# Attention tiles in a fused attention and MoE kernel: scores of one tile and the value product of the tile ahead in one run of small matmuls

## The chip, the core and the metric

The kernel runs on one core of a Trainium2 chip. The metric is the device time of one execution in microseconds, as a median over runs. The engines are PE (TensorE, matmuls and transposes; its weight loads are shown as PEld), DVE (VectorE), ACT (ScalarE), POOL (GpSimd) and SP, which here only issues DMAs. Each engine takes its instructions in the order of its own queue and waits on semaphores.

## What is computed

Chunked softmax attention, a dense MoE-like layer with a sigmoid-gated activation, and a layer of eight experts with routing:

```python
# q, k, v: (8, 8, 576, 64); chunks of 64 along the sequence
scores = scale * np.matmul(q_c, k_c.transpose(0, 1, 2, 4, 3))
scores = scores - np.max(scores, axis=-1, keepdims=True)
attn = np.exp(scores)
attn = attn / (np.sum(attn, axis=-1, keepdims=True) + 1e-09)
out = np.matmul(attn, v_c)
# x: (4608, 512), w_in (512, 2048), w_out (2048, 512)
h = x @ w_in
g = h * (1.0 / (1.0 + np.exp(-1.702 * h)))
x = g @ w_out
# routing: tokens with x @ w_skip > 0 go through their argmax expert
h = np.maximum(xc[mask] @ w1[e], 0.0)
y[mask] = gate_w[mask, None] * (h @ w2[e])
out[do_compute] = xc + y
```

## The kernel before, in words

The 4608 tokens are worked in nine blocks of 512 (NB = 9). A block's attention is four tiles of 128 tokens, each with two chunks and eight heads. The attention of block 0 is a prologue; that of block j + 1 runs inside the main loop of block j, between the big matmuls of the first MoE.

The main loop of a block has 16 steps (NF). Step i takes the 12 matmuls of `hps` (emit_h, line 269: 128x512, three products for each of four slices, as each operand is split into a high and a low part, xh and xl), then tanh on ACT and `sg` on DVE, `gh` on ACT and `gl` on DVE (emit_g), and the 12 matmuls of `yps` of the step ahead (emit_y, lines 289 to 293). Two banks of PSUM hold `hps`, four `yps`, and two, of the tag "at", all that attention and routing need. At a seam of two blocks the four `yps` are copied out as x2 by ACT and DVE (evac_y) and written to memory by SP, and x1, the attention's result, is split into xh (ACT casts) and xl (DVE) for the next block (split_x1). In a block's first eleven steps DVE also takes 36 dot products for the routing of the block ahead (line 326); late in the block a rank matmul `rk` takes a bank "at" (line 361). In block 0, `tick` converts the MoE weights from 64-bit numbers, on ACT, DVE and POOL.

A tile of attention has four stages in class Att: `a` transposes q and k (qTp and kTp, copied to qT and kT by ACT), `b` multiplies the scores (line 153, 16 products of 64x64, each two instructions in the trace) into two banks, `s0` and `s1`; DVE takes the maxima and the differences from these banks, and ACT the exp. `c0` normalises on DVE and `c1` transposes to pT. `d` is the product with the values (line 196, again 16 products) into two banks, `pv0` and `pv1`, from which ACT copies to x1. In the scores the bank is that of the operands' half of the rows; in the product too.

A table sets at which of the 16 steps a stage is emitted: STEPS = (0, 1, 3, 4), plus three for each further tile of the block (STEPS0 in block 0). `load_qk` of a tile is issued behind stage `a` of the tile ahead and `load_v` behind its stage `d`. The written order is not the final one: a scheduler of the framework orders the instructions of each engine by dependences and its own costs, so that a stage may move some steps, or be split with big matmuls in its middle.

Of the kernel before, what the change touches and what calls it, by code (L numbers as in the profile page):

```python
# [21 lines left out]
def kernel(  # L22
# [17 lines left out]
    NT, DM = out.shape  # L40
    DFF = w_in.shape[1]
    NE, _, FF = w1.shape
    P = 128
    CH = 64
    NHP = H // 2
    KD = DM // P
    NF = DFF // P
    BT = 512
    TPB = BT // P
    NB = NT // BT  # L50
# [7 lines left out]

    STEPS0 = (0, 1, 4, 5)
    STEPS = (0, 1, 3, 4)
    NXT = NT // SL + NE + NSING + 2
    BIG = float(1 << 20)

# [12 lines left out]
    def bank(shape, tag, name):  # L78
        return pp.tile(shape, F32, tag=tag, name=name, bufs=PB[tag])
# [28 lines left out]
    class Att:  # L108
# [34 lines left out]
                self.T.append(sb)  # L143

        def b(self):
            qT, kT = self.T
            ps = [bank([P, NHP, CH], self.tags[1], f"s{h2}") for h2 in range(2)]
            for hp in range(NHP):
                for c in range(2):
                    for h2 in range(2):  # L150
                        r = slice(h2 * CH, (h2 + 1) * CH)
                        cc = slice(c * CH, (c + 1) * CH)
                        PE.matmul(ps[h2][cc, hp, :], qT[r, hp, cc], kT[r, hp, cc], start=True, stop=True)

            self.p = qT.rearrange("p j (g k) -> p j g k", g=2)
            pw = self.p.rearrange("p (x h) g k -> p h g x k", h=2)
            self.st = ap.tile([P, NHP, 2], F32, tag="st", name="st", bufs=2)
            for h2 in range(2):
                DVE.tensor_reduce(self.st[:, :, h2], ps[h2], axis=AX.X, op=ALU.max)
            for h2 in range(2):  # L160
                DVE.tensor_tensor(
                    pw[:, h2], ps[h2].rearrange("p (g x) k -> p g x k", g=2),
                    self.st[:, :, h2:h2 + 1].rearrange("p (g x) o -> p g x o", g=2).to_broadcast(
                        [P, 2, 2, CH]), op=ALU.subtract,
                )
            ACT.activation(out=self.p, in_=self.p, func=AF.Exp, scale=float(D) ** -0.5)
# [15 lines left out]
            ACT.copy(out=self.pT, in_=ps)  # L182

        def d(self):


            ps = [bank([P, 2, P], self.tags[3], f"pv{g}") for g in range(2)]
            for x in range(2):
                for c in range(2):
                    for h2 in range(2):  # L190
                        for g in range(2):
                            r = slice(g * CH, (g + 1) * CH)
                            o = slice(h2 * CH, (h2 + 1) * CH)
                            cc = slice(c * CH, (c + 1) * CH)
                            j = 2 * x + h2
                            PE.matmul(ps[g][o, x, cc], self.v[r, c, j, :], self.pT[r, j, cc],
                                      start=True, stop=True)
            for g in range(2):
                ACT.copy(out=self.x1[g][:, :, self.col:self.col + P], in_=ps[g])


    whi, wlo = {}, {}
# [104 lines left out]
    def gate_load():  # L307
        SP.dma_start(out=wgT[:, :, 0:NE], in_=w_gate.rearrange("(k p) e -> p k e", p=P))
# [179 lines left out]
    def first_row(s):  # L488
        src = emeta[0:1, 1, s:s + 1] if s < NFIRST else meta[0:1, 0, s - NFIRST:s - NFIRST + 1]
        return SP.value_load(src, min_val=0, max_val=NROW - SL)  # L490
# [14 lines left out]
    def load_next():  # L505
        if cnt["load"] < len(wq):
            s, n, w = wq[cnt["load"]]
            cnt["load"] += 1
            single = s >= NFIRST + NPAIR and w == 0
            raw2.append((s, n, w, None if single else load_w2(expert(s), n, w)))  # L510
# [109 lines left out]
    def new_x1():  # L620
        return [mp.tile([P, 2, BT], F32, tag="x1", name="x1", bufs=2) for _ in range(2)]
# [22 lines left out]
    x1 = new_x1()  # L644
# [53 lines left out]
    xh, xl = split_x1(x1)  # L698

    fill, late = [], []  # L700
    wg = ws = None
    A = None
    slots = [Slot(s % 2, 2 if s < NFIRST + NPAIR else 1) for s in range(NS)]
    for j in range(NB):
        lastb = j + 1 == NB
        steps = {}
        if not lastb:
            x1 = new_x1()
            An = [Att((j + 1) * TPB + t, x1, t * P, ("at",) * 4, att_buf) for t in range(TPB)]
            for t in range(TPB):  # L710
                for n, kind in zip(STEPS if j else STEPS0, "abcd"):
                    steps.setdefault(3 * t + n, []).append((kind, t))
            if j == 0:
                An[0].load_qk()
                An[0].load_v()
            else:
                An[0].q, An[0].k, An[0].v = nxt_in
        else:
            rs.close()
            rawp = rs.enter_context(tc.tile_pool(name="raw", bufs=2, side="right", reuse_waits="tile"))  # L720
            for _ in range(4):
                load_next()
        ys = [bank([P, DM], "y", "yps") for _ in range(TPB)]
        prev = None
        nf = len(fill)
        for i in range(NF):
            steps.get(i, []).sort(key=lambda s: "acdb".index(s[0]))
            for kind, t in steps.get(i, ()):
                if kind == "c":
                    An[t].c0()  # L730
            sg = emit_h(i, xh, xl)
            span = NF // 2 - 2 if lastb else NF - 5
            nfill = -(-len(fill) // (span - i)) if i < span else 0
            if nfill:
                fill.pop(0)()
                nfill -= 1
            if j == 0:
                tick()
                if i == 7:
                    gate_load()  # L740
                elif i == 11:
                    gate_rows()
            g = emit_g(sg)
            if prev is not None:
                emit_y(i - 1, prev, ys)
            for kind, t in steps.get(i, ()):
                getattr(An[t], {"a": "a", "b": "b", "c": "c1", "d": "d"}[kind])()
                if kind == "a":
                    if t + 1 < TPB:
                        An[t + 1].load_qk()  # L750
                    elif j + 2 < NB:
                        nA = Att((j + 2) * TPB, None, 0, None, None)
                        nA.load_qk()
                elif kind == "d":
                    if t + 1 < TPB:
                        An[t + 1].load_v()
                    elif j + 2 < NB:
                        nA.load_v()
                        nxt_in = (nA.q, nA.k, nA.v)
            if j == 0:  # L760
                tick()
            for _ in range(nfill):
                fill.pop(0)()
            if late and (i >= span or late[0][0] < j):
                late.pop(0)[1]()
            if lastb:
                if prev is not None:
                    conv_next2()
                if i == NF // 2:
                    gstack.close()  # L770
                    m2 = ctx.enter_context(tc.tile_pool(name="m2", bufs=1, reuse_waits="tile"))
                    for s in range(NEARLY):
                        slots[s].list(first_row(s))
                if i >= NF // 2 + 2 and i - NF // 2 - 2 < NEARLY:
                    slots[i - NF // 2 - 2].gather((NB - 1) * BT)
            prev = g
        if j == 0:
            while tick_n[0] <= 2 * NF:
                tick()
            fstack.close()  # L780
            gstack = ExitStack()
            gp = gstack.enter_context(tc.tile_pool(name="gates", bufs=1, reuse_waits="tile"))
            wg = gp.tile([P, NE, DM], F32, name="wg")
            ws = gp.tile([P, DM], F32, name="ws")
            SP.dma_start(out=ws, in_=w_skip.rearrange("(o d) -> o d", o=1).to_broadcast([P, DM]))
            SP.dma_start(
                out=wg, in_=wgd[0:NE].rearrange("(o e) d -> o e d", o=1).to_broadcast([P, NE, DM]))
        if not lastb:
            xhn = split_x1(x1)
            emit_y(NF - 1, prev, ys)  # L790
            xh, xl = xhn
        else:
            slots[0].trans()
            emit_y(NF - 1, prev, ys)
            conv_next2()
        xs = evac_y(j, ys)
        lg = new_lg()
        if not lastb:
            fill = [lambda t=t, e=e, lg=lg, xs=xs: dot(lg, xs, t, e) for t in range(TPB) for e in range(NE + 1)]
            rt = route(j, lg)  # L800
            if j == NB - 3:
                rt.insert(3, order)
            late += [(j + 1, f) for f in rt]
# [108 lines left out]
```

## Time and profile before

| | us |
|---|---|
| median of 3 runs | 1247.73 (1245.55 to 1248.74) |
| profiled execution | 1246.55 |
| its span, first to last instruction | 1244.7 |
| PE busy (7984 matmul instructions) | 1194.9, 96% of the span |
| PE weight loads | 990.4 |
| DVE busy | 793.3 |
| ACT busy | 489.0 |
| POOL busy | 145.4 |

The busy time of an engine is a sum over stages that have different limits. The matmuls are pipelined: one that is shown with 0.39 us starts 0.23 us behind the one ahead of it, so it is the distance of the starts that tells what PE costs. "Idle before" in square brackets is time in which the engine stood still, with what released it.

### The profile page before, as it was taken

To read this page: it belongs to the slowest core of one execution; us is meant where nothing else is said; L and a number is where in the kernel's file an instruction comes from. 1 tells how busy PE (TensorE), PEld (TensorE's weight loads), DVE (VectorE), ACT (ScalarE), POOL (GpSimd) and SP (SyncE) were. 2 spreads that over 40 slices of the span, in tenths; PEclk is the share of its full clock that TensorE was granted. 3 is DMA by queue.
4 is the path that set the end of the run, shared out by engine and by line. 5 is a ranking of instruction groups with operands and counts; after the bars stand their busy time and mean duration, and the time that the engine had idled before them with its cause. 6 is when DMAs were issued, how large, how long until landed. Compare 5 with 4: busy or idle time off the path is not lost. (4 is left out here: it accounts for less than half of the span.)

```text
span 1244.7 us, 20848 instructions
## 1 busy us (share of the span) xinstructions
PE 1194.9 (96%) x7984; PEld 990.4 (80%) x7984; DVE 793.3 (64%) x1771; ACT 489.0 (39%) x825; POOL 145.4 (12%) x137
## 2 busy tenths in 40 slices
PE   6788999999999999999999999999999999999995
PEld 4566788878878887887887887788788999999885
DVE  5999477388359439548737835944884686666431
ACT  5866433243333333334334233333434444544320
POOL 2344000010000001001001000000103023132120
PEclk9999999999999999999999999999999999999998
DMA  9755241131122114113113112310524667667540
GB/s 220 207 159 159 53 154 37 34 94 35 34 81 48 26 27 111 35 26 95 42 35 94 26 43 61 69 26 9 186 86 152 216 186 258 212 222 236 190 152 9
DMA packets 181846, 128.99 MB, mean 104 GB/s; under 512 B 122335, under 2 KB 155359, under 8 KB 181616
## 3 DMA queue, kind: packets, MB, share of 16 engines
q1 hardware_dynamic: 177072, 117.09, 33.2%
q0 software_dynamic: 4672, 10.54, 2.5%
q8 instruction: 64, 1.05, 0.4%
q14 instruction: 38, 0.31, 0.1%
HBM read 103.59 MB, written 25.04 MB: 103 GB/s over the span
## 5 line engine op out<-in xcount | busy, mean ns | idle before, releaser
L269 PE MATMUL hps<-xh,whi 128*128 128x512 f32 x576 | 228.7, 400 | 6.5 <-DVE sg L273 5.9
L289 PE MATMUL yps<-whi,gh 128*128 128x512 f32 x576 | 229.6, 399 | 3.3 <-ACT gh L279 3.3
L269 PE MATMUL hps<-xl,whi 128*128 128x512 f32 x576 | 227.7, 395 | 3.5 <-DVE xl L259 3.5
L269 PE MATMUL hps<-xh,wlo 128*128 128x512 f32 x576 | 226.7, 394 | 0.0
L273 DVE SCALAR_TENSOR_TENSOR sg<-sg,hps 128x512 f32<-128x512 f32 x144 | 98.3, 684 | 201.4 <-ACT sg L272 200.6
L290 PE MATMUL yps<-wlo,gh 128*128 128x512 f32 x576 | 226.5, 393 | 0.0
L272 ACT ACTIVATE sg<-hps 128x512 f32<-128x512 f32 x144 | 85.5, 598 | 258.0 <-PE hps L269 244.7
L326 DVE CUSTOM_DVE_ANT_0 junk<-x,wg 128x512 f32<-128x512 f32 x256 | 176.3, 689 | 4.8
L516 DVE TENSOR_TENSOR elo<-rawe,ehi 128x1024 fp32r<-128x1024 f32 x88 | 107.5, 1223 | 88.3 <-ACT ehi L515 88.0
L293 PE MATMUL yps<-whi,gl 128*128 128x512 f32 x576 | 156.8, 393 | 0.7 <-DVE gl L280 0.7
L515 ACT CAST ehi<-rawe 128x1024 fp32r<-128x1024 f32 x88 | 92.2, 1049 | 144.1 <-PE h2p L581 70.3
L269 PEld LDWEIGHTS hps<-xh,whi 128*128 128x128 f32 x576 | 108.2, 189 | 31.0 <-DVE sg L273 8.4
L269 PEld LDWEIGHTS hps<-xl,whi 128*128 128x128 f32 x576 | 108.7, 189 | 27.3 <-DVE xl L259 5.2
L289 PEld LDWEIGHTS yps<-whi,gh 128*128 128x128 f32 x576 | 108.2, 188 | 27.4 <-ACT gh L279 4.3
L280 DVE SCALAR_TENSOR_TENSOR gl<-sg,gh 128x512 fp32r<-128x512 f32 x144 | 102.3, 710 | 42.1 <-ACT gh L279 39.5
L279 ACT ACTIVATE gh<-sg 128x512 fp32r<-128x512 f32 x144 | 91.0, 632 | 96.0 <-DVE sg L273 80.2
L269 PEld LDWEIGHTS hps<-xh,wlo 128*128 128x128 f32 x576 | 108.6, 189 | 22.5
L379 POOL DMA_INDIRECT tab<-pr,pos x36 | 42.2, 1172 | 713.1 <-DVE bs L369 519.8
L293 PEld LDWEIGHTS yps<-whi,gl 128*128 128x128 f32 x576 | 107.0, 188 | 23.2 <-DVE gl L280 1.3
L290 PEld LDWEIGHTS yps<-wlo,gh 128*128 128x128 f32 x576 | 108.2, 188 | 21.4
L581 PE MATMUL h2p<-xT,ehi 128*128 128x256 f32 x640 | 117.4, 283 | 0.0
L581 PEld LDWEIGHTS h2p<-xT,ehi 128*128 128x128 f32 x640 | 102.0, 191 | 2.6
(170 smaller groups left out, 1511.6 us busy)
## 6 DMA issues: line engine op xcount, KB each, us to landing
rawe<-in_moe_w_dram SPq DMA_DIRECT2D x88, 512.0 KB, 3.6
v<-in_v_dram SPq DMA_DIRECT2D x144, 64.0 KB, 2.5
x2d<-x SPq DMA_DIRECT2D x36, 256.0 KB, 5.8
out_dram<-x SPq DMA_DIRECT2D x36, 256.0 KB, 5.6
q<-in_q_dram SPq DMA_DIRECT2D x32, 256.0 KB, 3.1
k<-in_k_dram SPq DMA_DIRECT2D x32, 256.0 KB, 3.9
raw<-in_moe_w_in_dram SPq DMA_DIRECT2D x16, 512.0 KB, 4.8
raw<-in_moe_w_out_dram SPq DMA_DIRECT2D x16, 512.0 KB, 3.7
```

The lines of the kernel that those rows point to most:

```text
L269: PE.matmul(ps, a, b[:, kk], start=(n == 0), stop=(n == 3 * KD - 1))
L272: ACT.activation(out=sg, in_=ps, func=AF.Tanh, scale=0.851)
L273: DVE.scalar_tensor_tensor(sg, sg, 1.0, ps, op0=ALU.add, op1=ALU.mult)
L279: ACT.activation(out=gh, in_=sg, func=AF.Copy, scale=0.5)
L280: DVE.scalar_tensor_tensor(gl, sg, 0.5, gh.bitcast(F32), op0=ALU.mult, op1=ALU.subtract)
L289: PE.matmul(ys[t], gh[:, cs], wh, start=first, stop=False)
L290: PE.matmul(ys[t], gh[:, cs], wl, start=False, stop=False)
L293: PE.matmul(ys[t], gl[:, cs], wh, start=False, stop=last)
L326: DVE.tensor_tensor_reduce(junk, xs[t], wg[:, e, :] if e < NE else ws, 1.0, 0.0, ALU.mult, ALU.add, lg[:, t, e:e + 1])
L515: ACT.copy(out=hi, in_=raw)
L516: DVE.tensor_tensor(lo, raw, hi.bitcast(F32), op=ALU.subtract)
L581: PE.matmul(ps[:, f], a[:, c], self.xT[:, b, kk], start=(m == 0), stop=(m == 3 * KD - 1))
```

## The change

Attention from block 1 on becomes one stream of 32 tiles, `St`, over all blocks. The stages `b` and `d` are each cut into their matmuls (`b_mm`, `d_mm`) and what reads the banks (`b_post`, `d_post`). A function `burst` takes two banks of tag "at", each with the scores of one tile in its first half and the value product of the tile ahead in its second half: first the product's matmuls, then the scores' matmuls, then max, difference and exp of the scores, then the copies to x1. Bursts stand at steps 1, 4, 7, 10 and 13 of block 0, and at 1, 5, 9 and 13 of the blocks 1 to 7. A tile's transposes `a` come one step ahead of its burst, `c0` and `c1` two steps behind it, and its product in the next burst, three or four steps behind. The last burst has a product alone. `load_qk` of the next tile is issued behind `a`, `load_v` behind a tile's own burst. Lines move by 1 to 27: line 153 becomes 158, 196 becomes 207, 199 becomes 212, 269 becomes 296, 289 to 293 become 316 to 320.

```diff
-    STEPS0 = (0, 1, 4, 5)
-    STEPS = (0, 1, 3, 4)
+
+    BURSTS = {0: (1, 4, 7, 10, 13)}
+    BURSTN = (1, 5, 9, 13)
...
         def b(self):
+            ps = [bank([P, NHP, CH], self.tags[1], f"s{h2}") for h2 in range(2)]
+            self.b_mm(ps)
+            self.b_post(ps)
+
+        def b_mm(self, ps):
             qT, kT = self.T
-            ps = [bank([P, NHP, CH], self.tags[1], f"s{h2}") for h2 in range(2)]
...
+    def burst(nxt, old):
+
+
+        both = [bank([P, 4 * P], "at", f"sv{g}") for g in range(2)]
+        sc = [t[:, 0:2 * P].rearrange("p (h k) -> p h k", h=NHP) for t in both]
+        pv = [t[:, 2 * P:4 * P].rearrange("p (x k) -> p x k", x=2) for t in both]
+        if old is not None:
+            old.d_mm(pv)
+        if nxt is not None:
+            nxt.b_mm(sc)
+            nxt.b_post(sc)
+        if old is not None:
+            old.d_post(pv)
...
+    NST = NT // P - TPB
+    St = [Att(TPB + n, None, n % TPB * P, ("at",) * 4, att_buf) for n in range(NST)]
+    round_of = {}
+    for j in range(NB - 1):
+        for i in BURSTS.get(j, BURSTN):
+            round_of[j * NF + i] = len(round_of)
+    St[0].load_qk()
...
-            steps.get(i, []).sort(key=lambda s: "acdb".index(s[0]))
-            for kind, t in steps.get(i, ()):
-                if kind == "c":
-                    An[t].c0()
+            R = j * NF + i
+            nc_ = round_of.get(R - 2)
+            if nc_ is not None and nc_ < NST:
+                St[nc_].c0()
...
+            na = round_of.get(R + 1)
+            if na is not None and na < NST:
+                St[na].a()
+                if na + 1 < NST:
+                    St[na + 1].load_qk()
+            if nc_ is not None and nc_ < NST:
+                St[nc_].c1()
+            kb = round_of.get(R)
+            if kb is not None:
+                if kb:
+                    St[kb - 1].x1 = x1
+                burst(St[kb] if kb < NST else None, St[kb - 1] if kb else None)
+                if kb < NST:
+                    St[kb].load_v()
```

Over the whole kernel PE has its 1152 products of this kind in 84 runs before and in 43 now (eight of them in the prologue, in both); the transposes of q, k and p stand in 112 pieces before and in 134 now. Three places show how the order changes.

PE, burst of step 13 in block 1 of the new kernel (`sv_2541` and `sv_2542` are its two banks; line 207 is the product, line 158 the scores):

```order
L207 MATMUL sv_2541<-qT,v 64x64 [waits DMAHW7_49,Activation_49]
L207 MATMUL sv_2541<-qT,v 64x64
L207 MATMUL sv_2541<-qT,v 64x64 [waits DMAHW1_49]
L207 MATMUL sv_2541<-qT,v 64x64 x5
L158 MATMUL sv_2541<-kT,qT 64x64 x3
L207 MATMUL sv_2542<-qT,v 64x64 [waits DMAHW0_49,DVE_49]
L207 MATMUL sv_2542<-qT,v 64x64
L207 MATMUL sv_2542<-qT,v 64x64 [waits DMAHW2_49]
L207 MATMUL sv_2542<-qT,v 64x64 x5
L158 MATMUL sv_2542<-kT,qT 64x64 x3
L158 MATMUL sv_2541<-kT,qT 64x64
L158 MATMUL sv_2542<-kT,qT 64x64
```

Product and scores follow each other without a big matmul between them; in the bursts of this step in six blocks eight products and three scores of one bank stand together, since the other bank waits for DVE's copy of `rk`, while in the other bursts the two banks mostly take turns.

PE at the seam of blocks 1 and 2: before, the last product of the block ahead (line 196), the transposes of the next tile and the first matmuls of the new block.

```order
L196 MATMUL pv_2535<-qT,v 64x64
L196 MATMUL pv_2536<-qT,v 64x64
L140 MATMUL qTp<-ident,q 128x128 [waits DMAHW5_49,Activation_49]
L140 MATMUL qTp<-ident,q 128x128 x3
L140 MATMUL kTp<-ident,k 128x128 [waits DMAHW6_49,Activation_49]
L140 MATMUL kTp<-ident,k 128x128 x3
L269 MATMUL hps<-xh,whi 128x512 [waits Activation_49]
L269 MATMUL hps<-xh,whi 128x512
L269 MATMUL hps<-xl,whi 128x512 [waits DVE_49]
```

The same place of the new kernel, from the last `yps` matmuls of the step ahead to the first matmuls of the new block:

```order
L316 MATMUL yps<-whi,gh 128x512
L317 MATMUL yps<-wlo,gh 128x512
L316 MATMUL yps<-whi,gh 128x512
L317 MATMUL yps<-wlo,gh 128x512
L320 MATMUL yps<-whi,gl 128x512 [waits DVE_49]
L320 MATMUL yps<-whi,gl 128x512 x3
L141 MATMUL qTp<-ident,q 128x128 x3
L296 MATMUL hps<-xh,whi 128x512 [waits Activation_49]
L296 MATMUL hps<-xh,whi 128x512 [waits DVE_49]
L296 MATMUL hps<-xl,whi 128x512 [waits DVE_49]
```

The product that x1 needs no longer stands right ahead of the first matmul that reads xh: it is in the burst of step 13, with 36 big matmuls behind it.

ACT around a copy to x1, in block 1, before (line 199 copies, 272 is tanh, 279 is gh):

```order
L279 ACTIVATE gh<-sg 128x512 [waits DVE_49]
L199 COPY x_1713<-pv_2351 128x2x128 [waits PE_49]
L199 COPY x_1714<-pv_2352 128x2x128 [waits PE_49]
L272 ACTIVATE sg<-hps 128x512 [waits PE_49,Activation_49]
L279 ACTIVATE gh<-sg 128x512 [waits DVE_49]
L166 ACTIVATE qT<-qT 128x512 [waits DVE_49,PE_49]
```

And now (line 212 copies, 173 is exp, 299 is tanh, 306 is gh):

```order
L306 ACTIVATE gh<-sg 128x512 [waits DVE_49]
L212 COPY x_1757<-sv_2074 128x2x128 [waits DVE_49,PE_49]
L173 ACTIVATE qT<-qT 128x512 [waits DVE_49,PE_49,Activation_49]
L212 COPY x_1758<-sv_2075 128x2x128
L299 ACTIVATE sg<-hps 128x512 [waits PE_49]
L306 ACTIVATE gh<-sg 128x512 [waits DVE_49]
```

The first copy waits for DVE as well as for PE, the exp of the tile's scores has come between the two copies, and tanh and gh stand behind all three.

## Rows read from the trace of the kernel before

**Rows 1.** Busy time (and instructions) of each engine in two stretches.
```profile
49.00:122.00 73.00, 63.13 (x376) 48.08 (x376) 70.62 (x102) 52.99 (x95) 29.65 (x21) 1.00 0.55 167
262.00:363.00 101.00, 99.26 (x716) 79.78 (x715) 63.80 (x169) 34.30 (x64) 5.35 (x6) 1.00 0.21 53
```

**Rows 2.** Timeline of PE: start, duration, line, tiles, count; a run of 32.
```profile
300.13 0.39 PE L269 MATMUL hps<-xh,wlo 128*128 128x512 f32 x1
...
301.72 0.39 PE L269 MATMUL hps<-xh,whi 128*128 128x512 f32 x1
302.04 0.69 PE L153 MATMUL s<-kT,qT 64*64 64x64 f32 x32
302.66 0.50 PE L269 MATMUL hps<-xl,whi 128*128 128x512 f32 x1
303.00 0.39 PE L269 MATMUL hps<-xh,wlo 128*128 128x512 f32 x1
```

**Rows 3.** Timeline of PE, a run of 8.
```profile
370.87 0.39 PE L269 MATMUL hps<-xh,whi 128*128 128x512 f32 x1
371.19 0.34 PE L153 MATMUL s<-kT,qT 64*64 64x64 f32 x8
...
371.80 0.39 PE L269 MATMUL hps<-xh,wlo 128*128 128x512 f32 x1
```

**Rows 4.** Timeline of PE, 16 score matmuls of one bank.
```profile
132.48 0.68 PE L153 MATMUL s<-kT,qT 64*64 64x64 f32 x16
133.09 0.73 PE L293 MATMUL yps<-whi,gl 128*128 128x512 f32 x2
```

**Rows 5.** Timeline of PE, the last product, partly one bank at a time.
```profile
870.27 0.86 PE L196 MATMUL pv<-qT,v 64*64 64x64 f32 x32
871.06 1.20 PE L293 MATMUL yps<-whi,gl 128*128 128x512 f32 x4
```

**Rows 6.** Timeline of PE, scores and product in one run.
```profile
74.34 0.27 PE L153 MATMUL s<-kT,qT 64*64 64x64 f32 x2
74.35 0.27 PE L196 MATMUL pv<-qT,v 64*64 64x64 f32 x1
```

**Rows 7.** Timeline of PE, four transposes between big matmuls.
```profile
313.45 0.39 PE L269 MATMUL hps<-xh,wlo 128*128 128x512 f32 x1
313.69 0.60 PE L180 MATMUL pTp<-ident,qT 128*128 128x128 f32 x4
...
314.35 0.40 PE L269 MATMUL hps<-xl,whi 128*128 128x512 f32 x1
```

**Rows 8.** Waits of PE, 122 to 885 us: total, times, longest.
```profile
PE hps L269 <- DVE sg L273: 3.6, 8, 1.0
PE hps L269 <- DVE xl L259: 3.5, 4, 1.1
PE hps L269 <- ACT xh L258: 0.6, 1, 0.6
PE qTp L140 <- ACT x L199: 0.5, 1, 0.5
```

**Rows 9.** Busy times as in rows 1, then granted clock; behind the last seam.
```profile
874.00:878.00 4.00, 3.48 (x9) 2.75 (x10) 3.97 (x9) 0.88 (x2) 2.66 (x1) 0.58 0.61 213
```

**Rows 10.** Timeline of PE, ACT and DVE behind a run of scores.
```profile
249.92 0.60 ACT L272 ACTIVATE sg<-hps 128x512 f32<-128x512 f32 x1 [3.77 <-PE hps L269]
250.38 0.50 PE L289 MATMUL yps<-whi,gh 128*128 128x512 f32 x1
...
251.16 0.75 DVE L159 TENSOR_REDUCE st<-s 128x4 f32<-128x256 f32 x2
...
251.27 0.63 ACT L279 ACTIVATE gh<-sg 128x512 fp32r<-128x512 f32 x1 [0.76 <-DVE sg L273]
...
251.82 0.75 DVE L161 TENSOR_TENSOR qT<-s,st 128x256 f32<-128x256 f32 x2
```

**Rows 11.** Groups of DVE instructions, 122 to 870 us: busy us, mean ns.
```profile
L326 DVE CUSTOM_DVE_ANT_0 junk<-x,wg 128x512 f32<-128x512 f32 x224 | 154.3, 689 | 4.3
```

More of the change, by code (lines that the diff above doesn't have):

```diff
@@ L153, in b, with b_post @@
                         PE.matmul(ps[h2][cc, hp, :], qT[r, hp, cc], kT[r, hp, cc], start=True, stop=True)
-            self.p = qT.rearrange("p j (g k) -> p j g k", g=2)
+        def b_post(self, ps):
+            self.p = self.T[0].rearrange("p j (g k) -> p j g k", g=2)
             pw = self.p.rearrange("p (x h) g k -> p h g x k", h=2)
@@ L187, in d, with d_mm @@
             ps = [bank([P, 2, P], self.tags[3], f"pv{g}") for g in range(2)]
+            self.d_mm(ps)
+            self.d_post(ps)
+        def d_mm(self, ps):
             for x in range(2):
@@ L197, in d, with d_post @@
                                       start=True, stop=True)
+        def d_post(self, ps):
             for g in range(2):
                 ACT.copy(out=self.x1[g][:, :, self.col:self.col + P], in_=ps[g])
+    def burst(nxt, old):
[9 more added lines that the diff above has]
+            old.d_post(pv)
     whi, wlo = {}, {}
@@ L705 @@
         lastb = j + 1 == NB
-        steps = {}
         if not lastb:
             x1 = new_x1()
[L709 to L717, printed above, removed]
         else:
@@ L745 @@
                 emit_y(i - 1, prev, ys)
[L746 to L759, printed above, removed]
+            na = round_of.get(R + 1)
[12 more added lines that the diff above has]
+                    St[kb].load_v()
             if j == 0:
```

## Prediction

> **What bounds the kernel now.** I read the page's busy times first, which the table ahead gives: PE, the matmul engine, is busy for nearly all of the span. So the time is what PE does plus the little that it waits, and a change pays only where it shortens PE's own row of work or a wait of PE. Next the busy times by stretch, because that average hides two regimes [rows 1]. From 49 to 122 us, while the first block also converts the MoE weights, DVE is busy 70.62 of 73.00 us and PE 63.13: there DVE is the bound. From 122 us on PE is: 99.26 of 101.00 us in a later block, DVE 63.80.
>
> Then PE's rows one by one. In the main loop one 512-column matmul starts every 0.2275 us (seven from 300.13 to 301.72). A run of 32 small (64x64) matmuls stands between the big one that starts at 301.72 and the second big one after it, at 303.00 [rows 2]: 1.28 us where two big steps take 0.455, so 0.825 us for the run. A run of 8 takes 371.80 - 370.87 - 0.455 = 0.475 us [rows 3]. 24 more matmuls cost 0.35 us, or 0.0146 each; what is left, 0.475 - 8 x 0.0146 = 0.358 us, is paid for each run, however long: the small run starts 0.32 us after the last big matmul and the step behind the first big one is 0.34, both over 0.2275. This is the price the change works on. From 122 us on the trace has 67 such runs, the first at 132.48 [rows 4] and the last at 870.27 [rows 5]; a tile has 32 matmuls for its scores and 32 for its product, and 29 scores and 30 products are left by then, 1888 matmuls.
>
> **The change, part by part.** The sum is made against the profiled execution, 1246.55 us; its span is 1244.7 and the median of the runs shown is 1247.73, 1.18 above it.
>
> 1. *Fewer runs.* In the new order the 1888 small matmuls after 122 us stand in 31 runs: 29 bursts of 64 and the last product in pieces of 2 and 30. 67 - 31 = 36 runs fewer x 0.358 = 12.9 us. All of it lies on PE, which is the bound there. This takes the joint of products and scores inside a burst as free: at 74.34 two scores and, 0.01 us later, a product start together, in a run that the scheduler mixed [rows 6].
>
> 2. *Half-used array.* Where neighbours write one bank, they go half as fast: 16 scores of one bank take 0.61 us from their start to the next big matmul, 32 in two banks 0.62 [rows 2, 4]. For 16 in two banks I would expect 0.62 - 16 x 0.0146 = 0.39. Before there are four of these after 122 us (4 x 0.22 = 0.9 us) and three products that are partly so (0.79 instead of 0.62, 0.17 each, 0.5 us) [rows 2, 5]; all seven go. The new order brings six bursts of its own, one in each of six blocks, in which 8 products and 3 scores of one bank stand ahead of 8 and 3 of the other, because the rank matmul has just used that other bank. Each loses between 0.2 us (as the last run does) and 0.64 (44 matmuls x 0.0146, none overlapped); I take 0.5, as these stretches of one bank are longer than in that run, so nearer to the upper end: 3.0 us. Net 1.6 us lost.
>
> 3. *PE's waits.* [...] The waits for xh, xl and the x copy (0.6 + 3.5 + 0.5) come from the last product of a block, which the scheduler had put right ahead of the seam. Now it lies in the burst of step 13, 36 big matmuls (8.2 us) earlier, and behind the last hps PE has five transposes and twelve yps matmuls (5 x 0.11 + 12 x 0.2275 = 3.3 us) while ACT does a tanh and the first cast (0.60 each, by the tanh [rows 10]: an estimate, 1.2). They go, and with them, I take it, the low clock. The wait for sg, where a score bank of the MoE is held until DVE has copied x2 and done dots, is not touched: 3.6 / 8 = 0.45 each; eight seams, 3.6 us stay. For new waits at the shared banks (next part) I take 1.4 us, two dots of 0.69 [rows 11]. 9.8 - 3.6 - 1.4 = 4.8 us gained.
>
> 4. *What the shared banks add.* ACT's copies of x now wait for DVE too: both read the same bank, so the copy stands behind DVE's subtract, and behind the copy on ACT are exp, the second copy, then tanh and gh of the next step, for which PE waits in the end. DVE starts its reduces at 251.16, 0.8 us after the first big matmul behind the run of scores, 250.38, and is through with the subtracts 1.4 us later (251.82 + 0.75) [rows 10]. PE has 12 hps, 12 yps and 12 hps, 8.2 us, before it needs gh of the first of them. Tanh to the end of gh is 251.27 + 0.63 - 249.92 = 1.98 us [rows 10], two copies, by DVE's two subtracts of the same size, 0.75 and exp, by gh of the same size, 0.63: 3.4 us (estimates, both). 8.2 - 3.4 - 1.4 leaves 3.4 us, so DVE may reach the reduces 3.4 us behind the burst; today it is 0.8. That cover, 2.6 us or nearly four dots, is why I charge this edit little.
>
> 5. *Moves that cost nothing.* The transposes are cut up more (22 more pieces). Four take 314.35 - 313.45 - 0.455 = 0.445 us, 0.11 each, with no fixed part [rows 7]; a single one beside big matmuls isn't shown, and if each piece paid what a small run pays on entry (0.32 - 0.2275 [rows 2]), 22 x 0.09 = 2.0 us would be lost. The nearest row has none, so I take 0. Loads of q, k and v are issued by SP three or four steps (over 16 us) ahead, as before, and PE's waits after 122 us name no DMA [rows 8]; at a seam q goes ahead of the eight x2 writes on SP and k behind them, with four steps to spare. Spreading tiles over four steps instead of three takes one tile's scores out of the eleven steps that hold DVE's dots. Block 0 gets scores of one more tile, but after its conversions.
>
> 6. *Before 122 us.* Ten runs become five and two half-array pairs go: 5 x 0.358 + 4 x 0.22 = 2.7 us of PE. DVE is the bound and its work is the same, so between 0 and 2.7; near 0, as DVE idles for 2.4 us only: 0.7.
>
> Sum: 12.9 - 1.6 + 4.8 + 0.7 = 16.8. 1246.55 - 16.8 = 1229.75, and with 1.18 for the median **1230.9 us**.
>
> **Rivals.** *All waits go:* with no waits left at the seams, the six bursts at 0.2 and all of the 2.7 before 122 us, 3.6 + 1.4 + 6 x 0.3 + 2.0 = 8.8 more: 1222. For it: seams carry the waits and x arrives early. Against: dots and x2 copies still lie ahead of sg.
>
> *DVE takes the bound in the first eleven steps of a block*, where the dots are. Then the 21 bursts at steps 1, 5 and 9 of seven blocks shorten PE for nothing: 21 x 0.358 = 7.5 back, and 2 or 3 us of waits: 1241. For: 36 dots x 0.69 and eleven pairs of sg and gl fill most of those steps. Against: DVE is busy 63.80 of 101.00 [rows 1], and it now has one tile fewer there.
>
> *The joint costs what a switch costs:* then the change doesn't do what it says: 31 x 0.358 = 11.1 back, 1242. One mixed run speaks against it. [...]
>
> *Slower, by the shared bank:* if DVE reaches the reduces of the 21 bursts among dots later than the 3.4 us, ACT stands at the copy with tanh and gh behind it, and PE waits for every dot more. It decides against the change from (16.8 + 1.4) / 21 = 0.87 us a burst; two dots beyond the room, 1.4, give 21 x 1.4 = 29 and take the 1.4 with them: 1259. Against: the room is 2.6 us. [...]
>
> **How the numbers follow.** Forecast 1225 to 1237: 0.55. All waits go, 1218 to 1225: 0.14. DVE bound, 1237 to 1244: 0.17. Joint: 0.04. Slower: 0.05. Some of each with nothing left, 1244 to 1251.5: 0.05. 0.3% of the median, 3.7 us, is about what a measurement tells from no change; so faster means below 1244.0: 0.55 + 0.14 + 0.17 + 0.04 = 0.90, same 0.05, slower 0.05. The range 1219 to 1243 leaves out the tail of the second case, the slower one and nearly all of the last.
>
> **What would show it.** Step 1: some 43 runs in all; a burst of 64 takes 0.358 + 64 x 0.0146 = 1.29 us over two big steps. At 1.65 the joint is not free. Step 2: six bursts of 1.5 to 1.9. Step 3: no wait of PE for xl or xh at the seams, waits for sg near 0.45, and a clock of 1.00 around 870 us. Step 4: idle time of ACT's x copy ended by DVE's subtract, without PE waiting for gh. If PE waits for gh or sg in steps 5 to 13, step 4 is wrong; if the first block ends over 2 us earlier, step 6 is.

## The result and the profile after

The changed kernel takes 1226.76 us (median of 4 runs, 1225.83 to 1227.84) against 1246.86 us before (1245.55 to 1248.74): ratio 0.9843, 95% interval 0.9828 to 0.9858. That is 20.1 us less where 16.8 were forecast; the time is 4.1 us under the forecast 1230.9 and lies in the range. The profiled execution took 1227.84 us with a span of 1226.1. In a second comparison it was 1226.05 against 1249.20, ratio 0.9817 (0.9802 to 0.9831).

Busy times, instructions and granted clock in the stretches of [rows 1], in the kernel after:

```profile
49.00:122.00 73.00, 65.20 (x389) 50.66 (x388) 68.17 (x106) 54.29 (x98) 34.21 (x22) 0.98 0.61 177
262.00:363.00 101.00, 101.00 (x704) 83.16 (x703) 62.63 (x166) 34.90 (x64) 4.20 (x6) 1.00 0.20 53
```

In a later block PE now has no idle time at all (101.00 of 101.00). From the first stretch alone nothing can be said yet: its clock is 0.98, which comes up again below. The waits of PE from 122 to 885 us, which stand against [rows 8]:

```profile
PE hps L296 <- DVE sg L300: 1.8, 1, 1.8
PE yps L316 <- ACT gh L306: 0.5, 1, 0.5
```

Of 14 waits two are left. The timeline of PE (start, duration, line, tiles, count) round one of the bursts, against [rows 2, 3]:

```profile
293.95 1.07 PE L320 MATMUL yps<-whi,gl 128*128 128x512 f32 x4
294.95 0.69 PE L207 MATMUL sv<-qT,v 64*64 64x64 f32 x32
295.47 0.65 PE L158 MATMUL sv<-kT,qT 64*64 64x64 f32 x32
296.05 0.50 PE L296 MATMUL hps<-xh,whi 128*128 128x512 f32 x1
296.38 0.39 PE L296 MATMUL hps<-xl,whi 128*128 128x512 f32 x1
```

The last of the four yps starts at 294.63 (the burst begins 0.32 behind it, as in [rows 2]), the second hps at 296.38: 1.75 us, less two big steps of 0.2275, is 1.29 us for 64 small matmuls. The product ends and the scores begin without a pause.

Summed over the starts of PE's instructions, from the 250th big (128x512) matmul of hps and yps, counted from 0 (125.62 us before, 126.54 after), to the last yps:

| us beyond 0.2275 a big matmul | before | after |
|---|---|---|
| runs of small matmuls (67, 31), with 16 transposes beside them before and with the waits right behind them | 58.6 | 42.1 |
| transposes and rank matmuls that stand apart from runs | 43.8 | 44.4 |
| other gaps over 0.15 (waits, low clock) | 7.7 | 3.6 |
| the rest | 2.2 | 1.4 |
| stretch | 841.5 | 820.7 |

So 20.8 us were won in this stretch, for which 16.1 were forecast. About 1 us was lost ahead of it and 1.3 us behind it; behind it two executions of the kernel before differ by 2.4 us (277.58 and 279.97 us from the last yps to the end).

### The profile page after: what moved, and what is told of

Read it like the earlier page. It is cut to its first block, busy times and chain, and to the rows that moved or that the text cites. A ratio compares the mean times of both kernels' runs of the same rounds, so it can differ in the third digit from the quotient of the medians.

```text
span 1226.1 us, 20893 instructions
## 1 busy us (share of the span) xinstructions
PE 1182.7 (96%) x7984; PEld 991.8 (81%) x7984; DVE 783.9 (64%) x1771; ACT 490.2 (40%) x825; POOL 144.6 (12%) x137
## 5 line engine op out<-in xcount | busy, mean ns | idle before, releaser
L296 PE MATMUL hps<-xh,whi 128*128 128x512 f32 x576 | 231.6, 405 | 3.2 <-DVE sg L300 3.2
L307 DVE SCALAR_TENSOR_TENSOR gl<-sg,gh 128x512 fp32r<-128x512 f32 x144 | 99.0, 688 | 33.4 <-ACT gh L306 21.7
L406 POOL DMA_INDIRECT tab<-pr,pos x36 | 37.8, 1049 | 682.3 <-DVE st L166 335.0
```

Source lines behind the costliest of these rows:

```text
L296: PE.matmul(ps, a, b[:, kk], start=(n == 0), stop=(n == 3 * KD - 1))
L307: DVE.scalar_tensor_tensor(gl, sg, 0.5, gh.bitcast(F32), op0=ALU.mult, op1=ALU.subtract)
```

## Experiments

**The joint taken apart.** In 20 bursts the yps matmuls of the step stand between product and scores; banks and steps stay. `apart` is true at the burst steps from the second block on, `between` is called behind the product; at step 1 the scheduler keeps the burst in one run all the same.

```
-            if prev is not None:
+            if prev is not None and not apart:
                 emit_y(i - 1, prev, ys)
...
-                burst(St[kb] if kb < NST else None, St[kb - 1] if kb else None)
+                burst(St[kb] if kb < NST else None, St[kb - 1] if kb else None,
+                      (lambda: emit_y(i - 1, prev, ys)) if apart else None)
```

> The changed kernel with only the joint taken apart: in the 20 bursts of steps 5, 9 and 13 of the later blocks the yps matmuls of the step are written between the product and the scores, in the same two banks, with every tile at its step; 63 runs of small matmuls instead of 43, nothing else moved. Theory (a fixed 0.358 us for each run): 20 x 0.358 = 7.2 us more, 1226.8 + 7.2 = 1234.0. Rival (the gain came from the new steps and the emptied seams, the joint itself is worth little): 1226.8 within a microsecond.

Measured: 1237.62 us, ratio to before 0.992 (0.9904 to 0.9937), 10.9 above the changed kernel. The burst of above (its place and work are the same), timeline of PE:

```profile
294.76 0.39 PE L319 MATMUL yps<-wlo,gh 128*128 128x512 f32 x1
295.08 0.69 PE L207 MATMUL sv<-qT,v 64*64 64x64 f32 x32
295.71 1.19 PE L322 MATMUL yps<-whi,gl 128*128 128x512 f32 x4
296.83 0.69 PE L158 MATMUL sv<-kT,qT 64*64 64x64 f32 x32
297.46 0.50 PE L298 MATMUL hps<-xh,whi 128*128 128x512 f32 x1
```

The two halves take 0.827 and 0.830 us over two big steps, together 0.364 more than the burst in one piece: the fixed price of a run. In the seven bursts of step 9 it is 0.63, because the product alone is there written with neighbours of one bank (32 matmuls in 0.75 instead of 0.48 us from the first start to the last); in the six of step 13, which are cut behind 16 products, it is 0.51. 7 x 0.364 + 7 x 0.63 + 6 x 0.51 = 10.0. From the 300th big matmul to the last yps the kernel takes 816.01 us against 807.19, 8.8 more, and 10.4 more if the 1.6 us of low clock that the changed kernel has there (below) are left out of its time. The rival is out: every tile kept its step and its banks, and half of the gain was gone. The joint alone is 20 x 0.364 = 7.3 of it, as the theory has it; of the 3.7 by which the theory was short, 2.7 are the half-rate products that the edit brought with it.

**The last product back at the seam.** One line: `BURSTN = (1, 5, 9, 13)` becomes `(3, 7, 11, 15)`.

> The changed kernel with the bursts of the later blocks at steps 3, 7, 11 and 15, so that the last product of a block lies again right ahead of the seam (burst, 12 yps, then hps of the next block). 50 runs instead of 43: +7 x 0.358 = +2.5. The six bursts at half rate should go: -3.0. Theory (the seam waits vanished because the product moved away from it): PE waits again for xh, xl and the x copy, 4.6 us in all if as before and up to 1.4 x 8 = 11 more because the copy now stands behind DVE's subtract, and each low clock after a wait 1.6 more: 1231 to 1242. Rival (they vanished because DVE has one tile fewer among the dots): 1226.8 + 2.5 - 3.0 = 1226.3.

Measured: 1239.50 us, ratio 0.994 (0.9922 to 0.9958), 12.7 above the changed kernel and inside the theory's bounds. Waits of PE from 122 to 885 us:

```profile
PE hps L296 <- DVE xl L286: 6.4, 6, 1.1
PE kTp L141 <- ACT qT L189: 1.9, 6, 0.3
PE hps L296 <- DVE sg L300: 1.0, 1, 1.0
PE yps L316 <- ACT gh L306: 0.5, 1, 0.5
```

One seam, first PE, then ACT, then DVE:

```profile
357.83 0.65 PE L158 MATMUL sv<-kT,qT 64*64 64x64 f32 x32
...
361.52 0.73 PE L296 MATMUL hps<-xh,whi 128*128 128x512 f32 x2
363.33 0.50 PE L296 MATMUL hps<-xl,whi 128*128 128x512 f32 x1 [1.07 <-DVE xl L286]
```

```profile
359.70 0.38 ACT L212 COPY x<-sv 128x256 f32<-128x256 f32 x1 [2.95 <-DVE qT L168]
...
360.85 1.14 ACT L285 CAST xh<-x 128x512 fp32r<-128x512 f32 x2
```

```profile
361.33 1.28 DVE L326 COPY x<-yps 128x512 f32<-128x512 f32 x2
...
362.59 1.28 DVE L286 TENSOR_TENSOR xl<-x,xh 128x512 fp32r<-128x512 f32 x2
```

The chain is to be read backwards. PE waits for xl, and DVE takes xl only behind its two copies of x2 (361.33). The first cast of xh, which xl reads, was not done when they began (360.85, 0.6 us each). The casts stand behind ACT's copies of x, and the first of these, whose product was ready when the burst ended at 358.40, waited until 359.70 for DVE's subtract on the same bank. So two things meet at the seam, the shared bank and DVE's x2 copies; the run doesn't tell them apart. From step 13 the same chain costs nothing. The listed waits are 9.8 us instead of 2.3, and not all of the 12.7 us was traced. The rival, which gave the credit to DVE's lighter steps, had 1226.3.

**Six bursts at half rate.** At step 13 the changed kernel writes 16 products of one bank ahead of the other bank's (245.40 us, timeline of PE; the burst takes 1.797 us):

```profile
245.40 0.68 PE L207 MATMUL sv<-qT,v 64*64 64x64 f32 x16
...
246.09 0.51 PE L207 MATMUL sv<-qT,v 64*64 64x64 f32 x11
246.44 0.63 PE L158 MATMUL sv<-kT,qT 64*64 64x64 f32 x26
247.00 0.50 PE L296 MATMUL hps<-xh,whi 128*128 128x512 f32 x1
```

The first try starts the routing one step later and skips burst steps, which puts the rank matmul at step 14:

```
-            if late and (i >= span or late[0][0] < j):
+            if late and (kb is None or j > NB - 3) and (i >= span + (j < NB - 2) or late[0][0] < j):
```

> The changed kernel with the routing of the blocks started one step later and skipped in burst steps, so that the rank matmul leaves its bank free at step 13. 43 runs as before, all bursts with neighbours in two banks. Theory (the six bursts of 1.797 us cost 0.50 more because neighbours wrote one bank): six times 1.293, 6 x 0.50 = 3.0 us less, 1223.8. Rival (the 0.50 is the rank matmul's copy that the burst waits for): it moves with the rank matmul to another place, 1226.8.

Measured: 1226.25 us, ratio 0.9826 (0.9812 to 0.9840): no change. From the 300th big matmul to the last yps it takes 806.79 us against 807.19. The six bursts do take 1.293 now, but those of step 1 have gone from 1.293 to 1.58 and more: with the rank matmul at 14 the transposes of p slip behind it and those of k come up right ahead of the burst of step 1, whose second bank is then the late one. The loss moved, as the rival has it, though not for the rival's reason: the step-1 bursts show no wait, only 26 products ahead of the second bank's scores.

The second try spreads the dots over ten steps, so that the rank matmul stands at step 11:

```
-            span = NF // 2 - 2 if lastb else NF - 5
+            span = NF // 2 - 2 if lastb else NF - 6 if j else NF - 5
```

> The changed kernel with the dots of a block spread over ten steps instead of eleven, so that the routing starts a step earlier and the rank matmul stands at step 11, two steps ahead of the burst of step 13 and four big groups ahead of the next transposes. 43 runs as before. Theory (neighbours in one bank cost 0.50 in six bursts, and in the kernel with the rank matmul at step 14 the same loss came back as 0.29 in the bursts of step 1, whose second bank the late transposes still held): here every burst behind the first block takes 1.29 to 1.30 us, so 3.0 us less from 140 us to the last yps, 804.2 against 807.2 us. Rival (the bank pool always leaves one burst of a block with a late bank): one group of bursts of 1.58 or more, and the stretch within 1 us of 807.2.

Measured: 1222.73 us (1221.20 to 1225.29), ratio 0.9790 (0.9773 to 0.9808), beside 0.9817 for the changed kernel on the same chip; none of its five runs is as long as the shortest of the changed kernel's there (1225.47). The same burst:

```profile
244.03 0.69 PE L207 MATMUL sv<-qT,v 64*64 64x64 f32 x32
244.54 0.65 PE L158 MATMUL sv<-kT,qT 64*64 64x64 f32 x32
245.12 0.50 PE L296 MATMUL hps<-xh,whi 128*128 128x512 f32 x1
```

The stretch takes 803.21 us against 807.19, where 804.2 were expected: the six bursts give 3.0 and a low clock that did not come (the granted clock is 1.00 from 858 to 862 us; below) 1.6, while one burst took 1.1 longer than the others. The burst of step 1 in block 1, which takes 1.58 us in the changed kernel, keeps that in both tries. So the order of the matmuls is shown to be the cause of the 0.50. This version is the shortest, but 1.6 of the 4.0 us are the clock and not the edit.

**The room at the shared bank.** `NDUP` repeats of DVE's two reduces in 26 bursts, 0.75 us each:

```
-            for h2 in range(2):
+            for h2 in [0, 1] * (1 + (NDUP if self.t >= TPB + 6 else 0)):
                 DVE.tensor_reduce(self.st[:, :, h2], ps[h2], axis=AX.X, op=ALU.max)
```

> The changed kernel with DVE's two reduces of the scores done four times over in the last 26 bursts: 3 x 0.75 = 2.25 us more in which DVE holds both shared banks, ahead of ACT's copies. 49 runs instead of 43: +2.1. Theory (the room behind a burst is 3.4 us, DVE comes 0.8 to 1.4 late now): no wait of PE for gh or sg, so +2.1 alone, 1228.9. Rival (the shared bank is near its limit): each 0.75 beyond the room waits in 26 bursts, with a room of 1.4 already used up 26 x 2.25 = 58 us, 1285.

Measured: 1236.52 us, ratio 0.9891 (0.9871 to 0.9911), 9.8 above the changed kernel, where 2.1 were expected. PE's waits from 122 to 885 us are the two of the changed kernel, no more. The loss to the last yps is 5.8 us and lies in the bursts. One of them, the second piece of a burst that is now cut in two, timeline of PE:

```profile
321.35 0.51 PE L208 MATMUL sv<-qT,v 64*64 64x64 f32 x10
...
321.86 0.64 PE L159 MATMUL sv<-kT,qT 64*64 64x64 f32 x28
322.43 0.50 PE L297 MATMUL hps<-xl,whi 128*128 128x512 f32 x1
```

A block's bursts take 1.58, 1.57, 0.82 + 1.28 and 1.68 us, together 6.9 instead of 5.7: 7.5 over six blocks, 1.7 more than the 5.8, and about as much is the low clock (1.6 us) that the changed kernel has in this stretch (below). So DVE's lateness was not paid in waits but in the order of the small matmuls: where a bank is held longer, the scheduler writes one bank's matmuls ahead of the other's or cuts the burst.

PE was not spared by the room of 3.4 us. In the changed kernel DVE starts its reduces 0.1 to 2.2 us behind a burst and ends its subtracts 1.5 to 4.8 us behind it, as dots come in between; here the subtracts end 3.5 to 9.0 us behind it, while the prediction's room ends at 3.4 + 1.4 = 4.8. PE still doesn't wait for gh, because the order on ACT gives way: in the burst at 294.38 gh stands ahead of the copy.

```profile
301.42 0.63 ACT L307 ACTIVATE gh<-sg 128x512 fp32r<-128x512 f32 x1 [2.17 <-DVE sg L301]
302.69 0.37 ACT L213 COPY x<-sv 128x256 f32<-128x256 f32 x1 [0.65 <-DVE qT L169]
```

The other 4 us came behind the last yps, where the edit has no instruction: PE waits 3.1 us for gathers there instead of 1.6. The rest was not followed up.

> The same with the reduces done nine times over: 8 x 0.75 = 6.0 us more in each of 26 bursts. 64 runs instead of 43: +7.5. Theory (the room is 3.4 us and DVE comes 0.8 to 1.4 late): 6.0 + 1.4 - 3.4 = 4.0 us beyond the room; where it falls on PE in every burst, 26 x 4.0 = 104 and the time 1338; DVE's busy time in a block rises by 4 x 6.0 = 24 us to about 88 of 99, so it is not the bound by its sum. Rival (PE's order gives way, as ACT's copies are not needed before the next block, and only the added runs count): 1234.

Measured: 1346.04 us, ratio 1.0775 (1.0757 to 1.0794), mean clock 0.951. The figure is near the theory's, the place is another. Waits of PE from 118 to 1000 us, then PE and ACT at one seam:

```profile
PE hps L297 <- ACT xh L286: 85.2, 6, 15.8
...
PE yps L317 <- ACT gh L307: 0.5, 1, 0.5
```

```profile
387.78 1.22 PE L297 MATMUL hps<-xh,whi 128*128 128x512 f32 x2 [13.49 <-ACT xh L286]
...
390.18 0.63 PE L297 MATMUL hps<-xh,whi 128*128 128x512 f32 x1
390.61 0.63 PE L297 MATMUL hps<-xl,whi 128*128 128x512 f32 x1
```

```profile
386.70 0.37 ACT L213 COPY x<-sv 128x256 f32<-128x256 f32 x1 [14.37 <-DVE qT L169]
387.11 1.14 ACT L286 CAST xh<-x 128x512 fp32r<-128x512 f32 x2
```

The wait for gh, which the theory priced, stays at 0.5. The bursts slide towards the seam instead, and there the whole delay falls on xh at once; behind it a big matmul starts every 0.43 us (390.18, 390.61) instead of 0.2275, and from 360 to 400 us the mean granted clock is 0.79. That 26 x 4.0 comes near the sum of six such waits and their low clocks is chance.

**Dots out of step 0 of the last block,** with the rank matmul at 14 as above:

```
-            nfill = -(-len(fill) // (span - i)) if i < span else 0
+            nfill = -(-len(fill) // (span - i)) if i < span and not (lastb and i == 0) else 0
```

> As the one with the rank matmul moved, and besides no dots in step 0 of the last block, so that DVE comes to sg two dots (1.4 us) earlier there. Theory (PE's last wait at a seam, 1.84 us for sg at 861.03, is DVE's dots and x2 copies, and the low clock behind it follows from the wait): 1.84 - 1.4 = 0.4 left of the wait and no low clock, so 1.4 + 1.6 = 3.0 less than with the rank matmul moved alone: 1220.8. Rival 1 (the low clock has another cause): 1.4 less, 1222.4. Rival 2 (the dots moved to steps 1 to 5 make a new wait there): 1223.8 or more.

Measured: 1225.78 us, ratio 0.9822 (0.9807 to 0.9837), the same as without the edit. The timeline of DVE at the last seam shows why it tests nothing of the wait:

```profile
858.50 0.68 DVE L353 CUSTOM_DVE_ANT_0 junk<-x,wg 128x512 f32<-128x512 f32 x1
...
859.10 1.28 DVE L300 SCALAR_TENSOR_TENSOR sg<-sg,hps 128x512 f32<-128x512 f32 x2
```

Both dots, this one and one at 857.28, still stand ahead of sg: the scheduler places them when their x2 is ready, whatever step they are written in. The wait is 1.84 us again, but the granted clock behind it is 1.00 (859.8 to 864 us).

**Two kernels run once more.**

> The changed kernel itself once more. In its first profile the first block has a wait of 3.0 us for gh at 78.88, behind a raw weight load that landed late, and a low clock behind it; the kernels that share its first block word for word were through the 300th big matmul 1.4 us earlier. Theory (this wait belongs to that execution): the 300th big matmul at 138.6 instead of 140.04, no low clock at 80 us, and the stretch from there to the last yps 807.2 as before. Rival (it belongs to the order of the changed kernel): the wait is there again.

> The kernel before once more, for a second look at its first 140 us. Theory (the first block gives back what its five fewer runs and two fewer half-rate pairs take, about 1 to 2 us, and the late weight load hid it in the changed kernel's first profile): the 300th big matmul at 140.0 as in the first look, 1.4 to 1.9 us behind the undisturbed looks of the changed kernel (138.06 to 138.75), and the stretch from there to the last yps 827.1. Rival (the first block's time varies by as much in both kernels, so that nothing can be said of it): anywhere from 138 to 141.

The changed kernel: the 300th big matmul at 138.06 us instead of 140.04, without the long wait (0.98 us for gh at 77.46 instead of 2.99 at 78.88) and the low clock behind it (0.50 from 79.9 to 83.3 us in the first execution), though the mean granted clock of both executions is 0.993, and again 807.19 us from there to the last yps. The kernel before: 139.65 and 825.53 us (139.98 and 827.14 in its first profile). The late weight load is no matter of one execution, though: the kernel with the joint taken apart has the same first block and the same wait (2.95 us for gh at 78.16), and its 300th big matmul comes at 139.52. So the theory fails there; of eight executions with this first block two have the wait, 139.52 and 140.04, and six have not, 138.06 to 138.76. Without it the first block is 0.9 to 1.9 us shorter than before, with it there is hardly any gain. The 1.6 us by which the second execution of the kernel before is shorter behind 140 us is its clock at the last seam (window as in [rows 9]):

```profile
874.00:878.00 4.00, 3.82 (x17) 3.17 (x18) 3.93 (x11) 0.53 (x2) 3.36 (x1) 1.00 0.79 269
```

## Why the prediction held, step by step

1. *Fewer runs*: right in count and price. 31 runs from the 250th big matmul on; a burst of 64 takes 1.293 us (1.29 forecast), and the joint is free: one burst cut in two pays 0.364. By a joint that pays 0.358 too the change would have brought 31 x 0.358 = 11 us less.
2. *Half-used array*: six bursts at 0.50, as taken, and a seventh at 168.35 us, not forecast, with 0.29. The reason given was too narrow: not the rank matmul as such, but whichever transpose or rank matmul last takes a bank shortly ahead of the burst. Bank and half of the operands' rows always go together in this kernel, so the runs don't tell which of the two it is that makes neighbours go at half rate.
3. *PE's waits*: the way was right, the size was not. The 9.8 in the forecast's sum are the 8.2 us of the list [rows 8] and (1 - 0.58) x 4 = 1.6 us for the clock [rows 9]. From the 250th big matmul on, waits and low clock cost 11.4 us before (8.2 listed, 1.6 beyond the list, 1.6 for the clock) and 3.6 after: 7.8 us gained, not 4.8. This is the largest part of what the forecast fell short, and some of its errors cancel. The waits for xh, xl and x went, for the reason given. The waits for sg, taken to stay at 3.6, are gone at seven of eight seams. They were not only DVE's dots and x2 copies, as the prediction reads them: at four seams DVE itself stood idle for tanh (0.65 to 1.90 us),

```profile
372.86 0.69 DVE L273 SCALAR_TENSOR_TENSOR sg<-sg,hps 128x512 f32<-128x512 f32 x1 [0.65 <-ACT sg L272]
```

   and 14 to 32 scores in front of seven of the waits were too few to fill the time. Now PE has 64 matmuls there, the burst of step 1, which at 465.79 us fills the time from the last hps that has a bank until DVE is through with the first sg:

```profile
465.48 0.39 PE L296 MATMUL hps<-xh,wlo 128*128 128x512 f32 x1
465.79 0.69 PE L207 MATMUL sv<-qT,v 64*64 64x64 f32 x32
466.31 0.65 PE L158 MATMUL sv<-kT,qT 64*64 64x64 f32 x32
466.88 0.50 PE L296 MATMUL hps<-xh,whi 128*128 128x512 f32 x1
```

```profile
466.06 0.68 DVE L300 SCALAR_TENSOR_TENSOR sg<-sg,hps 128x512 f32<-128x512 f32 x1
```

   The seam of the last block, which has no burst, has a wait of 1.84 (0.96 before). That the burst is the cover is read from these rows and was not tested apart. New waits at the shared banks, taken as 1.4, did not come: the one new wait, 0.5 for gh at 123.68, lies in block 0. The low clock, said to vanish with the waits, stayed, from 861.5 to 865 us (columns as in [rows 9]):

```profile
861.50:865.00 3.50, 3.50 (x10) 2.70 (x9) 3.11 (x9) 0.73 (x2) 0.00 (x0) 0.51 0.90 340
```

   And the list of waits was priced too low. A wait is listed from the end of the matmul ahead (0.39 us long), while without it the next one would start 0.2275 behind that one's start:

```profile
858.80 0.39 PE L296 MATMUL hps<-xh,wlo 128*128 128x512 f32 x1
861.03 0.50 PE L296 MATMUL hps<-xh,whi 128*128 128x512 f32 x1 [1.84 <-DVE sg L300]
```

   861.03 - 858.80 - 0.2275 = 2.00 for a listed 1.84. So it is with six of the 14 waits before; the seven behind a run of small matmuls cost 0.07 to 0.10 beyond the list. Together that is the 1.6 above, of which 0.2 stays.
4. *Shared banks*: right in that no wait came, though not by the room. ACT's copy idles 5.06 us behind DVE's subtract at 299.45 us, and PE doesn't notice:

```profile
299.45 0.38 ACT L212 COPY x<-sv 128x256 f32<-128x256 f32 x1 [5.06 <-DVE qT L168]
```

   ACT idles for this copy behind DVE's subtract on the same bank 29 times from 122 to 885 us, 104.3 us in all. The room of 3.4 us with 2.6 to spare was no such margin: at step 1 the subtracts end 4.8 us behind the burst, where the room ends, and with the reduces done four times 9.0 us behind it, and PE waits for gh in neither. The rival's step that failed is the fixed order on ACT, tanh and gh behind the copy. What a longer hold of the banks costs is half-rate bursts first and a wait for xh at the seam then.
5. *Transposes cut up*: right. Those that stand alone cost 44.4 us with the rank matmuls instead of 43.8, of which four more of them are 0.4, although they come in 85 pieces instead of 61. In all the stretch has 344 instead of 356, one tile's twelve now lying ahead of it: 12 x 0.11 = 1.3 us of the table is moved, not won.
6. *Before 122 us*: not settled. The 250th big matmul comes at 125.62 and 125.28 us in two executions of the kernel before, and between 124.56 and 126.54 in eight with the changed first block. 0.7 us was forecast, and that is less than they differ among themselves.

The measured 1226.76 lies about midway between the forecast and the rival *All waits go* (1222). Of that rival the waits came true, but not its six bursts at 0.2 or, in the profiled execution, its shorter first block.

## What to carry to other kernels

Small matmuls among big ones are paid by the run (0.358 us each here): count runs, price one from a long and a short one, and join what can stand together even if two kinds of work then share a bank. Before joining, look at who else takes a bank right ahead of the run, since a bank that comes late makes the small matmuls of the other go at half rate (0.50 us a burst here) without showing as a wait. A run that cannot be removed can be put where PE would wait.

## What the runs showed of the hardware that was not expected

- The same wait is followed by a low clock in some executions and not in others. Behind the 1.84 us at the last seam the granted clock is 0.51 in the changed kernel (861.5 to 865 us) and 0.70 in the kernel with the rank matmul at 14 (861 to 865); behind the same wait it is 1.00 with the dots out of step 0 besides (859.8 to 864) and with the rank matmul at 11 (858 to 862). The kernel before has 0.58 in one execution and 1.00 in the other (874 to 878). In the changed kernel eight steps from 861.63 to 865.01 us take 3.38 us instead of 8 x 0.2275 = 1.82: 1.6 us. What decides it is not shown. A forecast can count such a microsecond neither as kept nor as won.
- One burst of the best version, at 440.97 us, took 2.37 us instead of 1.29. The timeline of PE shows a pause in its scores with no releaser, and two other kernels have one such burst at another place (2.40 at 759.96, 2.46 at 760.58). Its cause stays open.

```profile
441.49 0.93 PE L158 MATMUL sv<-kT,qT 64*64 64x64 f32 x23
442.83 0.38 PE L158 MATMUL sv<-kT,qT 64*64 64x64 f32 x9 [0.41 <-issue]
```
